# Attention and a two-layer GELU network on one core: second layers ordered behind the next first layer, and zero products in two waits of TensorE

## The chip, the cores and the metric

The kernel runs on one core of a Trainium2 chip. Five engines work side by side: TensorE (PE: products, and PEld: its weight loads), VectorE (DVE), ScalarE (ACT), GpSimd (POOL) and SyncE (SP, which starts most of the DMAs). The metric is the device time of one execution in microseconds (us); less is better.

## The reference, cut to what matters

```python
# attention: batch 4, 8 heads, 768 positions, head size 64; local window 96, 8 global columns
scores = scale * q @ k.T + bias            # masked to local or global positions
a = exp(scores - max) ; a = a / (sum(a) + 1e-9)
x = (a @ v)  -> [3072 tokens, 512]
# network
h = x @ w_in                               # [3072, 2048]
g = 0.5 * h * (1.0 + erf(h / sqrt(2)))
out = g @ w_out                            # [3072, 512]
```

## The kernel before, in words

The 3072 tokens are cut into 12 chunks of 256, three to a batch. The 2048 hidden columns are cut into 8 slices of 256. A step is one pair (chunk, slice); `STEPS` lists 99 entries: first the two first chunks in turn slice by slice, with three empty entries for a delay, then (2, 0) to (2, 7), (3, 0) and so on to (11, 7). The weights come in as 64-bit words and are taken apart on ScalarE and VectorE during the first two chunks, so that stage is crowded; later chunks find the weights split in a high and a low part in SBUF.

One step has a first layer (`m1`, lines 489, 493, 495: sixteen products in two halves f = 0, 1, of 128x512 and 128x256), a reduction of its bank on VectorE (line 497), two GELU passes on ScalarE for a high part `gh` and an exact value `gr` (lines 516, 517), the low part `gl` on VectorE (line 177), and a second layer (`m2`, line 536: twelve products of 512 columns, six for each half k of the tokens, adding to `acc` in PSUM). After slice 7 ScalarE copies `acc` out (line 549) and starts the DMA to HBM.

The attention of a later chunk runs between these steps: `scores_pair` (line 347), `exps`, `flip` (transposes, line 398, then ScalarE copies them to `pt`, line 402) and `av_pair` (line 430), whose result goes through ScalarE and VectorE into `x`, as a high and a low part; the low part is the last one written.

The loop in `run` emits for each T, in this order: the flag (at T = 91 alone), loads, `m1` of step T + 1 with its GELU, the transposes, the values, the scores, `m2` of step T, and the exponentials. This order is a priority and not the final order. A planner simulates the engines and puts each engine's instructions in a queue: at each moment the first ready one in the order of the code. Each engine then runs its queue in that order on the chip. `after(ins, prev, why)` adds an edge for the planner alone: `ins` comes behind `prev`. `behind` does so for VectorE, behind the last reduction or `gl` so far. Banks of PSUM for scores, transposes, values, first layers and the flag come from one pool of six (`bank`), and each is taken when the planner places the first instruction that writes it.

The flag (lines 622 to 645) is a small check of the inputs' range. Its last steps are three comparisons on VectorE, placed by `behind` after the `gl` of step 91, that is (11, 0); a reduction (line 639); and a transpose on TensorE into a bank (line 641). `warm` (line 366) puts products with zeros (`wz`) on TensorE at the start and between the scores of the first chunks; their results are read by nobody.

Of the kernel before, what the change touches and what calls it, by code (L numbers as in the profile page):

```python
# [17 lines left out]
P = 128  # L18
# [3 lines left out]
NP = H // 2  # L22
# [9 lines left out]
NST = 8  # L32
# [18 lines left out]
DECODE.update({(1, i): i - 1 for i in range(4)})  # L51
DECODE.update({(s, i): 2 * s - 2 + i // 2 for s in range(2, NST) for i in range(4)})
FILL = {(0, 0, 0): 8, (0, 0, 1): 5, (0, 1, 1): 9, (0, 2, 1): 4, (0, 3, 1): 4, (1, 0, 1): 4}
LATE = 6
CAT = 2
NEGMASK = -1000000000.0
# [30 lines left out]
class Fast:  # L87
# [107 lines left out]
    def split_weights(self, s, i):  # L195
        nc = self.nc
        if i == 0:
            if s == LATE:
                self.early.close()
# [120 lines left out]
    def scores_pair(self, c, p):  # L320
# [9 lines left out]
        for j in range(2):  # L330
            for a in range(1 if c == 0 and j == 0 else 2):
                for hh in range(2):
# [17 lines left out]
                    prev = ins  # L350
            if (c, p, j) in FILL:
                prev = self.warm(FILL[c, p, j], prev)
        for hh in range(2):
# [7 lines left out]
                self.last_dve = ins.ins  # L361
            self.pt_n[c, 2 * p + hh] = nn

    def warm(self, n, prev=None):
        for i in range(n):
            ins = self.nc.tensor.matmul(self.warm_ps, lhsT=self.wz[:, 0:P], rhs=self.wz, start=True, stop=True).ins  # L366
            if prev is not None:
                self.after(ins, prev, "between the products of the first attention")
            prev = ins
        return prev  # L370
# [22 lines left out]
    def flip(self, c, h):  # L393
        nc = self.nc
        nn = self.pt_n.pop((c, h))
        tp = self.bank([P, 3, P], f"t{c}_{h}")
        for i, o in enumerate((0, 2 * P, NK if c % CPB == 0 else P)):
            nc.tensor.transpose(tp[:, i, :], nn[:, o:o + P], self.ident)  # L398
        if h % 2 == 0:
            self.ptp2 = self.ptp.tile([P, 2, 3, P], F32, name=f"pt{c}_{h}", tag="pt")  # L400
        pt = self.ptp2[:, h % 2]
        nc.scalar.copy(pt, tp)  # L402
        self.pt_t[c, h] = pt

    def av_pair(self, c, p):

        nc = self.nc
        first = c % CPB == 0
        if p == 0:
            self.x[c] = self.xp.tile([P, NP, 2, CT], F32R, name=f"x{c}", tag="x")  # L410
        if c:
            if p % 2 == 0:
                return
            ps = range(p - 1, p + 1)
        else:
            ps = range(p, p + 1)
        n = len(ps)
        quarters = c > CAT
        if quarters:
            rows = [self.bank([P, 2, n, P], f"av{c}_{p}_{r}") for r in range(2)]  # L420
        elif first:
            avb = self.bank([P, 2, n, P], f"av{c}_{p}")
            av = [avb[:, j] for j in range(2)]
        else:
            av = [self.bank([P, n, P], f"av{c}_{p}_{j}") for j in range(2)]
        heads = {(i, hh): (self.pt_t.pop((c, 2 * q + hh)), self.vr[c][:, :, (2 * q + hh) * D:(2 * q + hh + 1) * D])
                 for i, q in enumerate(ps) for hh in range(2)}

        def add(out, lhs, rhs, start, stop):
            ins = nc.tensor.matmul(out, lhsT=lhs, rhs=rhs, start=start, stop=stop, skip_group_check=True).ins  # L430
            if self.last_av is not None:
                self.after(ins, self.last_av, "heads and halves in turn")
            self.last_av = ins

        for i in range(n if quarters else 0):
            for j in range(2):
                for r in range(2):
                    ks = slice(r * HQ, (r + 1) * HQ)
                    for hh in range(2):
                        pt, vt = heads[i, hh]  # L440
                        add(rows[r][hh * D:(hh + 1) * D, j, i, :], vt[ks, j, :], pt[ks, j, :],
                            i == 0 and j == 0, r == 1 and (first or j == 0) or r == 0 and j == 1 and not first)
        for i in range(0 if quarters else n):
            for j in range(2):
                for hh in range(2):
                    pt, vt = heads[i, hh]
                    add(av[j][hh * D:(hh + 1) * D, i, :], vt[:, j, :], pt[:, j, :],
                        i == 0 and (j == 0 or not first), first and j == 0)
        for i in range(n):
            for a in range(2):  # L450
                for j in range(2):
                    if first and j == 0:
                        continue
                    ks = slice(0, HQ) if first else slice(j * HQ, (j + 1) * HQ)
                    for hh in range(2):
                        pt, vt = heads[i, hh]
                        qs = slice(a * HQ, (a + 1) * HQ)
                        o = rows[0 if first else j][:, j] if quarters else av[j]
                        add(o[hh * D:(hh + 1) * D, i, qs], vt[ks, 2 + a, :], pt[ks, 2, qs], False, True)
        if quarters:  # L460
            xs = self.sm.tile([P, 2, n, P], F32, name=f"xs{c}_{p}", tag="o", bufs=3)
            nc.scalar.copy(xs, rows[1])  # L462
            nc.vector.tensor_tensor(out=xs, in0=rows[0], in1=xs, op=ALU.add)
            xh, xl = (self.x[c][:, ps.start:ps.stop, e].rearrange("d p (j q) -> d j p q", j=2) for e in range(2))
            nc.scalar.copy(xh, xs)
            self.lo_dve(xl, xs, xh)
            return
        if first:
            xh, xl = (self.x[c][:, ps.start:ps.stop, e].rearrange("d p (j q) -> d j p q", j=2) for e in range(2))
            nc.scalar.copy(xh, avb)  # L470
            self.lo_dve(xl, avb, xh)
            return
        for j in range(2):
            xh, xl = (self.x[c][:, ps.start:ps.stop, e, j * P:(j + 1) * P] for e in range(2))
            nc.scalar.copy(xh, av[j])
            self.lo_dve(xl, av[j], xh)

    def m1(self, t, f):
        nc = self.nc
        c, s = STEPS[t]  # L480
        x = self.x[c]
        wh, wl = self.win[s]
        fs = slice(f * P, (f + 1) * P)
        if c >= CAT:
            if f == 0:
                self.h[t] = self.hs.tile([P, 2, CT], F32, name=f"hs{t}", tag="hs")
            hp = self.bank([P, 2, CT], f"h{t}_{f}")
            for d in range(NP):
                nc.tensor.matmul(hp.rearrange("p e t -> p (e t)"), lhsT=wh[:, d, fs],  # L489
                                 rhs=x[:, d].rearrange("p e t -> p (e t)"),  # L490
                                 start=d == 0, stop=d == NP - 1, skip_group_check=True)
                if d:
                    nc.tensor.matmul(hp[:, 0, :], lhsT=wl[:, d - 1, fs], rhs=x[:, d - 1, 0, :],  # L493
                                     start=False, stop=False, skip_group_check=True)
            nc.tensor.matmul(hp[:, 0, :], lhsT=wl[:, NP - 1, fs], rhs=x[:, NP - 1, 0, :],  # L495
                             start=False, stop=True, skip_group_check=True)
            self.last_dve = nc.vector.tensor_reduce(out=self.h[t][:, f, :], in_=hp.rearrange("p e t -> p t e"),  # L497
                                                    axis=mybir.AxisListType.X, op=ALU.add).ins
            return
        if f == 0:  # L500
            self.h[t] = self.bank([P, 2, CT], f"h{t}")
        hp = self.h[t]
        n = 0
        for d in range(NP):
            for w, e in ((wh, 0), (wh, 1), (wl, 0)):
                nc.tensor.matmul(hp[:, f, :], lhsT=w[:, d, fs], rhs=x[:, d, e, :],  # L506
                                 start=n == 0, stop=n == 3 * NP - 1)
                n += 1
# [12 lines left out]
    def m2(self, t, k):  # L521
        nc = self.nc
        c, s = STEPS[t]
        gh, gl = self.g[t]
        wh, wl = self.wout[s]
# [5 lines left out]
        acc = self.acc[c, k]  # L531
        ks = slice(k * P, (k + 1) * P)
        n = 0
        for f in range(2):
            for g, w in ((gh, wh), (gh, wl), (gl, wh)):
                nc.tensor.matmul(acc, lhsT=g[:, f, ks], rhs=w[:, f, :],  # L536
                                 start=s == 0 and n == 0, stop=s == NST - 1 and n == 5)
                n += 1
        if s == NST - 1:
            o = self.sm.tile([P, DM], F32, name=f"o{c}_{k}", tag="o", bufs=3)  # L540
# [281 lines left out]
```

## Time and profile before

| | |
|---|---|
| Time, median of 3 runs | 683.29 us (682.39 to 683.58) |
| The profiled execution | 682.04 us |
| its span, from the first to the last instruction | 680.2 us |
| TensorE busy, weight loads | 665.6 us (98%), 561.5 us (83%) |
| VectorE, ScalarE, GpSimd busy | 390.3, 364.6, 102.4 us (57%, 54%, 15%) |
| Chain that ended last | PE 94%, DVE 3%, ACT 2% |
| Mean granted clock of TensorE | 0.997 of full speed |

Times within the trace are counted from the first instruction. Products overlap in the pipeline of TensorE: what one costs in a stream is the distance from its start to the next start, which is less than its listed duration. In a row of instructions in order of time the first number is the start, the second the duration of the row (of all its instructions together), and a bracket at the end gives the idle time ahead of it and what ended that.

### The profile page before, as it was taken

The numbers are of one execution on the slowest core, as the hardware profiler recorded it, in microseconds if no ns is written. First come the engines' busy times: TensorE is split into PE (matmuls) and PEld (weight loads), VectorE is DVE, ScalarE is ACT, GpSimd is POOL, SyncE is SP. The second block draws the span as 40 slices with busy tenths as digits, with TensorE's granted clock in tenths as the row PEclk, the third lists the DMA queues.
The fourth block names the chain that finished last, engine by engine and source line by source line (L and its number), as shares of the span: only waits on it lengthen the run. The fifth ranks groups of instructions, "written<-read, shape, count | busy, mean of one in ns | idle before, by whom it ended". The sixth has DMA issues, their size and how long they took to land.

```text
span 680.2 us, 13571 instructions
## 1 busy us (share of the span) xinstructions
PE 665.6 (98%) x5215; PEld 561.5 (83%) x5215; DVE 390.3 (57%) x1136; ACT 364.6 (54%) x852; POOL 102.4 (15%) x232
## 2 busy tenths in 40 slices
PE   8989999999999999999999999999999999999996
PEld 6658898988888888888888888888888888888784
DVE  5989989334555654655555555555546555453432
ACT  3796687554654645536636537446456356363211
POOL 3100330310301301301201121031031031010000
PEclk9999999999999999999999999999999999999998
DMA  8945944241531613403514324224154052000001
GB/s 267 276 147 186 290 152 125 79 125 47 164 94 62 164 35 122 140 29 113 126 41 153 97 67 156 69 72 140 32 132 135 24 161 64 32 1 16 16 1 36
DMA packets 66183, 71.21 MB, mean 105 GB/s; under 512 B 32704, under 2 KB 49344, under 8 KB 66112
## 3 DMA queue, kind: packets, MB, share of 16 engines
q1 hardware_dynamic: 61664, 62.93, 30.6%
q10 hardware_dynamic: 4448, 7.34, 3.1%
q8 instruction: 43, 0.70, 0.4%
q14 instruction: 28, 0.23, 0.1%
HBM read 63.97 MB, written 6.29 MB: 103 GB/s over the span
## 4 chain that ended last, share of the span: by engine, by line
PE 94%; DVE 3%; ACT 2%; issue 0%; DVEq 0%
PE acc L536 40%; PE h L489 22%; PE h L493 8%; PE h L506 6%; PE av L430 5%; PE s L347 5%; PE t L398 4%; PE h L495 3%; PE warm_ps L366 1%; DVE n L358 1%; DVE n L388 1%; ACT w L209 0%; ACT n L379 0%; DVE wb L217 0%; ACT L516 0%
## 5 line engine op out<-in xcount | busy, mean ns | idle before, releaser
L489 PE MATMUL h<-x,winh 128*128 128x512 f32 x640 | 216.3, 400 | 0.0
L497 DVE TENSOR_REDUCE hs<-h 128x256 f32<-128x512 f32 x160 | 107.7, 685 | 99.5 <-PE h L495 98.9
L536 PE MATMUL acc<-wouth,gh 128*128 128x512 f32 x384 | 156.8, 408 | 2.2 <-ACT gh L516 2.2
L536 PE MATMUL acc<-woutl,gh 128*128 128x512 f32 x384 | 150.3, 392 | 0.0
L536 PE MATMUL acc<-wouth,gl 128*128 128x512 f32 x384 | 148.5, 393 | 0.1
L388 POOL TENSOR_SCALAR n<-n,su 128x192 f32<-128x192 f32 (+1 forms) x160 | 71.3, 464 | 438.3 <-ACT n L379 217.9
L177 DVE TENSOR_TENSOR gl<-gr,gh 128x512 fp32r<-128x512 f32 x96 | 67.5, 703 | 117.6 <-ACT gr L517 117.6
L493 PE MATMUL h<-x,winl 128*128 128x256 f32 x480 | 134.7, 281 | 0.0
L489 PEld LDWEIGHTS h<-x,winh 128*128 128x128 f32 x640 | 114.2, 188 | 20.4 <-issue 0.3
L516 ACT ACTIVATE gh<-hs 128x512 fp32r<-128x512 f32 x80 | 50.7, 633 | 125.6 <-DVE hs L497 122.1
L402 ACT COPY pt<-t 128x384 f32<-128x384 f32 x96 | 45.4, 479 | 112.8 <-PE t L398 109.5
L493 PEld LDWEIGHTS h<-x,winl 128*128 128x128 f32 x480 | 90.4, 188 | 7.2
L536 PEld LDWEIGHTS acc<-wouth,gh 128*128 128x128 f32 x384 | 72.2, 188 | 21.0 <-ACT xs L462 3.9
L536 PEld LDWEIGHTS acc<-wouth,gl 128*128 128x128 f32 x384 | 72.1, 188 | 17.0 <-issue 0.6
L536 PEld LDWEIGHTS acc<-woutl,gh 128*128 128x128 f32 x384 | 72.3, 188 | 12.3
L379 ACT ACTIVATE n<-n,mn 128x192 f32<-128x192 f32 (+1 forms) x144 | 62.3, 434 | 1.4 <-DVE mn L358 1.2
L358 DVE CUSTOM_DVE_ANT_0 n<-s,pen 128x192 f32<-128x192 f32 (+1 forms) x192 | 54.6, 340 | 2.2 <-PE s L347 2.2
L517 ACT ACTIVATE gr<-hs 128x512 f32<-128x512 f32 x80 | 49.3, 616 | 0.0
L506 PE MATMUL h<-x,winh 128*128 128x256 f32 x256 | 48.9, 286 | 0.4 <-ACT x L470 0.2
L398 PE MATMUL t<-ident,n 128*128 128x128 f32 x288 | 47.2, 274 | 1.2 <-DVE n L388 1.2
L430 PE MATMUL av<-pt,vr 64*64 64x64 f32 (+2 forms) x1312 | 42.8, 249 | 2.7 <-ACT pt L402 2.6
L495 PE MATMUL h<-x,winl 128*128 128x256 f32 x160 | 45.2, 282 | 0.0
(87 smaller groups left out, 738.2 us busy)
## 6 DMA issues: line engine op xcount, KB each, us to landing
w<-w SPq DMA_DIRECT2D x32, 512.0 KB, 5.0
c<-w SPq DMA_DIRECT2D x32, 512.0 KB, 5.3
out<-o ACTq DMA_DIRECT2D x23, 256.0 KB, 2.0
qr<-qT SPq DMA_DIRECT2D x11, 512.0 KB, 3.9
vr<-v SPq DMA_DIRECT2D x22, 256.0 KB, 4.2
kr<-kT SPq DMA_DIRECT2D x16, 320.0 KB, 5.0
vr<-v SPq DMA_DIRECT2D x19, 192.0 KB, 2.8
kr<-kT SPq DMA_DIRECT2D x36, 64.0 KB, 4.1
```

The lines of the kernel that those rows point to most:

```text
L177: return self.nc.vector.tensor_tensor(out=out, in0=in_, in1=hi.bitcast(F32), op=ALU.subtract)
L358: ins = nc.vector.tensor_tensor_reduce(out=nn[:, j * NK:j * NK + n], in0=sp[hh][:, j, 0:n], in1=pen, scale=-slope(2 * p + hh), scalar=3e38 ...
L379: self.table(nc.scalar.activation(out=nn, in_=nn, func=AF.Exp, bias=mn[:, i:i + 1], scale=-1.0, accum_out=su[:, i:i + 1]))
L388: ins = eng.tensor_scalar(out=nn, in0=nn, scalar1=su[:, i:i + 1], scalar2=0.0, op0=ALU.mult, op1=ALU.add)
L398: nc.tensor.transpose(tp[:, i, :], nn[:, o:o + P], self.ident)
L430: ins = nc.tensor.matmul(out, lhsT=lhs, rhs=rhs, start=start, stop=stop, skip_group_check=True).ins
L489: nc.tensor.matmul(hp.rearrange("p e t -> p (e t)"), lhsT=wh[:, d, fs], rhs=x[:, d].rearrange("p e t -> p (e t)"), start=d == 0, stop=d == ...
L493: nc.tensor.matmul(hp[:, 0, :], lhsT=wl[:, d - 1, fs], rhs=x[:, d - 1, 0, :], start=False, stop=False, skip_group_check=True)
L495: nc.tensor.matmul(hp[:, 0, :], lhsT=wl[:, NP - 1, fs], rhs=x[:, NP - 1, 0, :], start=False, stop=True, skip_group_check=True)
L497: self.last_dve = nc.vector.tensor_reduce(out=self.h[t][:, f, :], in_=hp.rearrange("p e t -> p t e"), axis=mybir.AxisListType.X, op=ALU.ad ...
L506: nc.tensor.matmul(hp[:, f, :], lhsT=w[:, d, fs], rhs=x[:, d, e, :], start=n == 0, stop=n == 3 * NP - 1)
L536: nc.tensor.matmul(acc, lhsT=g[:, f, ks], rhs=w[:, f, :], start=s == 0 and n == 0, stop=s == NST - 1 and n == 5)
```

## The change

Three edits. (1) For second layers of chunks from 3 on, the first product of each half k is ordered behind the last first-layer product of the following step. (2) In the values of pair 3 of chunk 0, three products of zeros are put into the bank, behind the transposes before. (3) In the transposes of head 6 of chunk 1, two products of zeros are put into the bank, behind the transposes of head 5. The zeros are overwritten by the products that follow in the same bank.

```diff
+FILL_T = {(1, 6): 2}
+FILL_AV = {(0, 3): 3}
...
+    def zeros(self, n, out):
+        prev = self.last_t
+        for i in range(n):
+            ins = self.nc.tensor.matmul(out, lhsT=self.wz[:, 0:P], rhs=self.wz[:, 0:out.shape[1]],
+                                        start=True, stop=True, skip_group_check=True).ins
+            self.after(ins, prev, "behind the transposes of the head before")
+            prev = ins
...
         tp = self.bank([P, 3, P], f"t{c}_{h}")
+        if (c, h) in FILL_T:
+            self.zeros(FILL_T[c, h], tp.rearrange("k i q -> k (i q)"))
         for i, o in enumerate((0, 2 * P, NK if c % CPB == 0 else P)):
-            nc.tensor.transpose(tp[:, i, :], nn[:, o:o + P], self.ident)
+            self.last_t = nc.tensor.transpose(tp[:, i, :], nn[:, o:o + P], self.ident).ins
...
             avb = self.bank([P, 2, n, P], f"av{c}_{p}")
             av = [avb[:, j] for j in range(2)]
+            if (c, p) in FILL_AV:
+                self.zeros(FILL_AV[c, p], avb.rearrange("d j n q -> d (j n q)"))
...
-            nc.tensor.matmul(hp[:, 0, :], lhsT=wl[:, NP - 1, fs], rhs=x[:, NP - 1, 0, :],
-                             start=False, stop=True, skip_group_check=True)
+            self.last_m1 = t, nc.tensor.matmul(hp[:, 0, :], lhsT=wl[:, NP - 1, fs], rhs=x[:, NP - 1, 0, :],
+                                               start=False, stop=True, skip_group_check=True).ins
...
             for g, w in ((gh, wh), (gh, wl), (gl, wh)):
-                nc.tensor.matmul(acc, lhsT=g[:, f, ks], rhs=w[:, f, :],
-                                 start=s == 0 and n == 0, stop=s == NST - 1 and n == 5)
+                ins = nc.tensor.matmul(acc, lhsT=g[:, f, ks], rhs=w[:, f, :],
+                                       start=s == 0 and n == 0, stop=s == NST - 1 and n == 5).ins
+                if n == 0 and c > CAT and self.last_m1[0] == t + 1:
+                    self.after(ins, self.last_m1[1], "behind the first layer of the next step")
                 n += 1
```

## Rows read from the trace of the kernel before

**Rows 1.** The page: busy us, share of the span and count, TensorE alone.

```profile
...
PE 665.6 (98%) x5215; PEld 561.5 (83%) x5215; DVE 390.3 (57%) x1136; ACT 364.6 (54%) x852; POOL 102.4 (15%) x232
...
```

**Rows 2.** Waits of TensorE, whole span: who for whom, us, times, longest.

```profile
...
PE av L430 <- ACT pt L402: 2.6, 3, 1.3
PE acc L536 <- ACT gh L516: 2.2, 2, 1.4
...
```

**Rows 3.** Waits of TensorE from 0 to 62 us.

```profile
...
PE acc L536 <- ACT gh L516: 0.8, 1, 0.8
...
```

**Rows 4.** TensorE in order of time around the last wait.

```profile
...
624.22 0.63 PE L489 MATMUL h<-x,winh 128*128 128x512 f32 x2
...
625.38 0.40 PE L536 MATMUL acc<-wouth,gh 128*128 128x512 f32 x1
...
629.68 0.27 PE L495 MATMUL h<-x,winl 128*128 128x256 f32 x1
...
631.40 0.50 PE L536 MATMUL acc<-wouth,gh 128*128 128x512 f32 x1 [1.45 <-ACT gh L516]
...
634.60 0.27 PE L641 MATMUL flag_ps<-ident,bad 128*1 128x128 f32 x1
634.63 0.71 PE L489 MATMUL h<-x,winh 128*128 128x512 f32 x2
...
```

**Rows 5.** VectorE and ScalarE in order of time, the same stretch.

```profile
...
623.81 0.69 DVE L177 TENSOR_TENSOR x<-xs,x 128x512 fp32r<-128x512 f32 x1 [0.69 <-ACT x L465]
...
628.36 0.59 ACT L549 COPY o<-acc 128x512 f32<-128x512 f32 x1 [0.79 <-PE acc L536]
...
630.71 0.63 ACT L516 ACTIVATE gh<-hs 128x512 fp32r<-128x512 f32 x1 [1.77 <-DVE hs L497]
...
631.90 0.69 DVE L177 TENSOR_TENSOR gl<-gr,gh 128x512 fp32r<-128x512 f32 x1 [1.22 <-ACT gr L517]
...
632.81 0.16 DVE L639 TENSOR_REDUCE bad<-ok 128x1 f32<-128x5 f32 x1
...
```

**Rows 6.** TensorE and VectorE in order of time, an undisturbed step.

```profile
...
659.73 0.63 PE L489 MATMUL h<-x,winh 128*128 128x512 f32 x2
...
662.41 0.28 PE L495 MATMUL h<-x,winl 128*128 128x256 f32 x1
662.53 0.40 PE L536 MATMUL acc<-wouth,gh 128*128 128x512 f32 x1
...
664.64 0.69 DVE L177 TENSOR_TENSOR gl<-gr,gh 128x512 fp32r<-128x512 f32 x1 [1.22 <-ACT gr L517]
...
665.27 0.61 PE L489 MATMUL h<-x,winh 128*128 128x512 f32 x2
...
```

**Rows 7.** In order of time, chunk boundary 3 to 4, the first of five.

```profile
...
252.65 0.69 DVE L177 TENSOR_TENSOR x<-xs,x 128x512 fp32r<-128x512 f32 x1
...
255.30 0.40 PE L536 MATMUL acc<-wouth,gh 128*128 128x512 f32 x1
...
```

**Rows 8.** TensorE in order of time, the first chunks.

```profile
...
1.46 5.49 PE L366 MATMUL warm_ps<-wz 128*128 128x512 f32 x12 [1.46 <-DVE wz L572]
...
12.25 2.35 PE L366 MATMUL warm_ps<-wz 128*128 128x512 f32 x9
...
30.00 0.43 PE L430 MATMUL av<-pt,vr 128*64 128x128 f32 x2 [1.33 <-ACT pt L402]
30.36 0.88 PE L347 MATMUL s<-kr,qr 64*64 64x192 f32 x16
...
47.59 0.76 PE L398 MATMUL t<-ident,n 128*128 128x128 f32 x4 [1.19 <-DVE n L388]
...
```

**Rows 9.** Three stretches: length, busy us of each engine, granted clock (PEclk), DMA.

```profile
core 0: us, PE busy (x) PEld busy (x) DVE busy (x) ACT busy (x) POOL busy (x), PEclk, DMA share, GB/s
28.00:30.00 2.00, 0.67 (x5) 0.35 (x5) 2.00 (x6) 2.00 (x8) 0.00 (x0) 1.00 0.96 291
46.00:48.00 2.00, 0.81 (x6) 0.51 (x5) 1.97 (x8) 2.00 (x8) 0.00 (x0) 1.00 0.00 0
30.00:40.00 10.00, 9.52 (x95) 7.08 (x96) 9.99 (x39) 8.48 (x19) 0.00 (x0) 1.00 0.80 305
```

## The prediction, made before the changed kernel was run

> **What bounds the kernel now.** I read the page's busy table first, then the waits of TensorE, then its instructions in order of time around each wait, then the other engines beside those. The reader is to see in the busy table that TensorE is occupied for 665.6 us, 98% of the span [rows 1]. So time can leave only in three ways: TensorE gets less to do, its instructions follow each other more tightly, or one of its waits goes. The change takes no product away, so it comes down to the waits and to the places beside them. The waits are few: three for copied probabilities (2.6 us together), two of a second layer for its GELU (2.2 us together) [rows 2], one of 1.19 us before a head's transposes [rows 8], and the start. In the first 62 us a GELU is waited for once, for 0.8 us [rows 3]; the list of waits from 60 to 620 us is empty. So one wait is left behind the first stage, the 1.45 us before 631.40 in the last chunk [rows 4].
>
> The profiled execution took 682.04 us, of which 680.2 are the span; the median of the three timed runs is 683.29, so 1.25 above it. I make the sum against 682.04 and carry that offset along.
>
> **The tie, where the order changes.** With step numbers t over all (chunk, slice) pairs, the tie asks that the second layer of t starts behind the last product of the first layer of t + 1. From the fourth chunk on the stream of TensorE already has that order nearly everywhere. I find it broken at six chunk boundaries: at five, two or three of the twelve second-layer products stand in the middle of the next chunk's first layer; at the sixth (chunk 10 to chunk 11), all twelve.
>
> The first of the five is at 255.30. There TensorE has no gap, so moving two products behind ten costs and brings nothing, provided that the first layer's inputs are there when it is no longer interrupted. The low half of x is written by 253.34 (252.65 + 0.69) and needed at 255.30 [rows 7], so 1.96 us to spare: cost 0. What fails if that cover goes is a wait of the same size as the delay, five times.
>
> **The sixth boundary, where time is to be had.** In the kernel before, the first layer of (11, 0) stops after six products at 625.38, twelve second-layer products of (10, 7) run, then the other ten; the last is issued at 629.68 [rows 4]. Now TensorE has nothing left that the order allows: the next second layer is that of (11, 0) itself, whose GELU can only start now (630.71 [rows 5]). It starts at 631.40, runs in two halves, and the next thing (the transpose of the flag) is issued at 634.60 [rows 4]. Without trouble the first product would have followed 0.12 us after 629.68 (662.41 to 662.53) and the twelve would take 2.74 us (662.53 to 665.27) [rows 6]. So this place costs 634.60 - 629.80 - 2.74 = 2.06 us, of which 1.45 is the wait that the list names and the rest is the slow start and a second stop for gl.
>
> With the tie the first layer of (11, 0) runs in one piece: 2.80 us (659.73 to 662.53 [rows 6]) from 624.22, so to 627.02. The low half of x is there at 624.50 [rows 5] and wanted at 625.38: 0.88 us to spare. Then the twelve products of (10, 7), to 629.76, and beside them the reduction and the GELU of (11, 0). In an undisturbed step gl is complete 2.92 us after the last first-layer product (662.41 to 665.33 [rows 6]); here that is 626.90 + 2.92 = 629.82.
>
> What is late next is the flag. The code asks for the flag's bank before the banks of the first layer of (11, 1), and the stream shows that banks are given out in the order of the code: the flag's transpose at 634.60, then that first layer at 634.63 [rows 4]. The transpose is queued on TensorE ahead of the first layer of (11, 1), and by the tie ahead of the second layer of (11, 0) as well; both wait for it. It needs the flag's last reduction on VectorE, which is ordered behind gl and ended 0.38 us after it (632.59 to 632.97 [rows 5]). So it is ready at about 630.20, and TensorE is free at 629.76: a wait of 0.44 us, with 0.16 for the signal and the slow start after a stop (an estimate: a quarter of the 0.61 by which this place now costs more than its wait) 0.6 us in all. From there on first and second layers alternate without a wait, as in the step of [rows 6]. **Gain of the tie: 2.06 - 0.6 = 1.46 us.** Its bounds: 2.06 if the flag is in time, and a loss if the GELU is not in time (rivals). The output copies of chunk 10 move some 1.6 us later with their second layer; they and their DMA on ScalarE's queue are waited for by nobody near. No load moves, and nothing is passed on the queues of SP or POOL.
>
> **The products with zeros.** Three of 256 columns go into the bank of the fourth pair's values in chunk 0, behind the last transposes; the wait there is 28.67 to 30.00. Two of 384 columns go into the bank for head 6 of chunk 1; the wait there is 46.40 to 47.59 [rows 8]. A zero product of 512 columns takes 2.35 / 9 = 0.26 us [rows 8]; by that the three cost at most 0.78 and the two at most 0.52, and both fit into their waits. If either bank is not free by then, the products go onto the path: +1.3 us is the upper end. At both moments the scores of the pair before have been read out and at most four of the six banks are held (the two transposes' and values not yet copied), so I take 0.
>
> Below nothing: taking the bank early also lets the tiles behind it take theirs. After the wait the two value products come first and the sixteen scores of the next pair right behind (30.00, 30.36 [rows 8]); with the bank taken at 28.7 the scores may run inside the wait, which would give back at most their 0.88 us. But in the stretch after it VectorE is busy 9.99 of 10 us [rows 9], so an earlier score mostly makes a longer later wait. Between 0 and 0.88 I take the end near VectorE's full row: **-0.2 us**.
>
> As for the clock: the granted clock is 1.00 in both waits [rows 9], the upper of its two levels (2.4 GHz), so in this execution the zeros keep up nothing that had fallen. The Trainium skill ("TensorE: Matmul & The Clock Gate", Part 1, on what is actually happening) says that the throttled state is the default and activity releases it, and that one kernel shows different counts of slow first products from run to run. By that the timed runs may hold a fall which this profile does not show; no row here has one. It is a rival below.
>
> **Sum.** 682.04 - 1.46 - 0.2 = 680.4 for a profiled execution; with the offset of 1.25, a median of 681.6 us.
>
> **The rivals.**
> *The wait changes its name.* ScalarE takes the first output copy of chunk 10 ahead of the GELU of (11, 0). That copy can start 0.24 us after its six products (628.36 against 625.38 + 2.74 for the later one [rows 4, 5]), so at 627.02 + 1.37 + 0.24 = 628.63, ending 629.22; from GELU start to complete gl is 1.88 us (630.71 to 632.59), then 0.38 for the flag: 631.48. The wait is 1.72 + 0.16, the gain 0.2: 683.1. For it: before, both copies stood ahead of that GELU. Against: there it became ready long after them; now its input is there first and it stands first in the code.
> *Slower.* Both copies ahead of it: the second ends at 629.76 + 0.24 + 0.59 = 630.59, gl at 632.47, flag 632.85; TensorE waits 3.09 + 0.16 = 3.25 us where it lost 2.06, with the second layer that used to fill the time now tied behind. The kernel gets 1.2 us slower: 684.5. It decides from the point where the flag is ready later than 631.66.
> *The timed runs lose clock in the first waits, and the zeros stop that.* At the lower level twelve products take 5.49 us, 0.46 each, against 0.26 [rows 8]; 2.8 us of products issued at that level would be the whole offset of 1.25. Then the median comes down by it too: 681.6 - 1.2 = 680.4. For it: two of the three runs stand 1.2 and 1.5 us above the profiled one. Against: every row of the granted clock there.
> *The zeros don't get into their waits*, or shift the order of the crowded first 60 us: +1.3 on the sum, 682.9.
>
> **How the numbers follow.** Forecast 0.52 (681.6, its own range 680.8 to 682.4), first rival 0.15, slower 0.09, clock 0.12, zeros outside 0.12. A measurement of this kernel tells a change from none at about 0.2%, here 1.4 us: faster means below 681.9, slower above 684.7. Of the forecast about 0.37 lies below 681.9, with the clock rival all but 0.01: faster 0.48. Slower by 0.2% takes the slow rival with something of the zeros or a bad median: 0.06. The rest, 0.46, is within. The range 680.1 to 683.5 leaves out most of the slow rival and the ends of the others.
>
> **What would show it.** Right: the second layers of the last chunk no longer list the 1.45 us wait for gh; the first layer of (11, 0) is in one piece from 624; TensorE's wait there is about half a microsecond and names the flag's transpose. Wrong: that transpose waits over 1.5 us; a first layer waits for x at a boundary; the two waits at 28.7 and 46.4 have grown, or a zero product stands behind their end; TensorE's count of waits between 60 and 620 us is no longer none.

## The result, and the profile after

The changed kernel took 685.73 us in the median of eight runs (685.07 to 689.07), the kernel before 683.02 (eight runs, 682.39 to 683.88): ratio 1.0053, 95% interval 1.004 to 1.0066, so by the ratio 3.6 us slower (the medians alone are 2.7 us apart, since three of the eight runs lie some 3 us above the other five). The forecast was 681.6, range 680.1 to 683.5: wrong in sign and outside its range. The eight runs form two groups, five from 685.07 to 686.00 and three from 688.08 to 689.07. The profiled execution, 688.08 with a span of 686.2, is of the upper group and shows both losses.

TensorE's row of the page hardly changed from [rows 1]: the change added no work worth speaking of.

```profile
...
PE 667.2 (97%) x5220; PEld 564.0 (82%) x5220; DVE 389.3 (57%) x1136; ACT 365.2 (53%) x852; POOL 113.8 (17%) x232
...
```

TensorE's waits in the whole span (who for whom, us in total, times, longest) did change.

```profile
...
PE s L349 <- POOL qr L173: 3.2, 1, 3.2
PE t L410 <- DVE n L398: 2.2, 3, 1.4
PE h L520 <- ACT x L489: 1.8, 1, 1.8
PE h L520 <- DVE x L179: 1.5, 2, 1.2
...
PE acc L550 <- ACT gh L530: 1.2, 2, 0.7
PE flag_ps L657 <- DVE bad L655: 1.1, 1, 1.1
PE av L444 <- ACT pt L414: 0.7, 1, 0.7
```

The two targets shrank against [rows 2]: `pt` from 2.6 to 0.7, `gh` from 2.2 to 1.2. The third, for `n`, grew from 1.2 to 2.2 in three pieces. New are the flag's and, 6.5 us together, those for `x` and `qr`: tiles that the diff doesn't touch.

Where the time goes is read from the starts of first layers, counted in both traces in order of time (us):

| | before | after | difference |
|---|---|---|---|
| first of the 24-product groups of chunks 0 and 1 | 31.17 | 29.50 | -1.67 |
| third | 55.07 | 52.26 | -2.81 |
| fourth | 60.47 | 63.58 | +3.11 |
| seventh | 79.18 | 82.27 | +3.09 |
| eighth | 85.85 | 93.88 | +8.03 |
| step (2, 0) | 148.60 | 156.18 | +7.57 |
| step (11, 0) | 624.22 | 631.74 | +7.52 |
| step (11, 5) | 654.17 | 660.80 | +6.62 |

The kernel is ahead until 55 us, loses around 58 and again around 88, carries 7.5 us unchanged through nine chunks, and gets 0.90 back in the last chunk. The -2.81 overstates the lead, because six products of the third group now stand ahead of value products that came before it: chunk 1's last value products end at 54.90 and not at 55.14, with those six products (0.8 us) already done, so the lead is about 1.0 us. From there to +3.11 the first place costs about 4.1 us; the second costs 8.03 - 3.09 = 4.94. So there are three places to read.

**First place.** TensorE in order of time from 27.5 us: the zeros lie inside the old wait, and the rest closed up behind them. The sixteen scores and the next first layer now run before the values, which no longer wait (in [rows 8] the order was 1.33 us of wait, values, scores).

```profile
...
28.16 0.60 PE L369 MATMUL av<-wz 128*128 128x256 f32 x3
28.69 0.88 PE L349 MATMUL s<-kr,qr 64*64 64x192 f32 x16
29.50 0.50 PE L520 MATMUL h<-x,winh 128*128 128x256 f32 x2
...
30.76 0.92 PE L444 MATMUL av<-pt,vr 128*64 128x128 f32 x12
```

Some 25 us later ScalarE's order differs. Before (lines L475 and L229 there), then after (L489, L231, L211):

```profile
...
55.17 0.65 ACT L475 CAST x<-av 128x256 fp32r<-128x256 f32 x2 [1.71 <-PE av L430]
55.70 0.64 ACT L229 CAST winh<-wb 128x512 fp32r<-128x512 f32 x1
...
```

```profile
...
54.93 0.37 ACT L489 CAST x<-av 128x256 fp32r<-128x256 f32 x1 [1.91 <-PE av L444]
55.20 0.62 ACT L231 CAST winh<-wb 128x512 fp32r<-128x512 f32 x1
55.72 0.68 ACT L211 ACTIVATE w<-w 128x512 int32<-128x512 uint32 x1
56.28 0.37 ACT L489 CAST x<-av 128x256 fp32r<-128x256 f32 x1
...
```

Two instructions on weights now stand between the two copies of chunk 1's last values, and on VectorE four others stand before the second low part (55.68 to 57.81). TensorE's queue waits for both:

```profile
...
56.71 0.39 PE L520 MATMUL h<-x,winh 128*128 128x256 f32 x1 [1.81 <-ACT x L489]
58.28 0.58 PE L520 MATMUL h<-x,winh 128*128 128x256 f32 x1 [1.19 <-DVE x L179]
...
62.55 0.50 PE L550 MATMUL acc<-wouth,gh 128*128 128x512 f32 x1 [0.69 <-ACT gh L530]
...
```

The granted clock falls in the same stretch. Windows of after (length, busy us of PE, PEld, DVE, ACT, POOL, granted clock, DMA), then of before:

```profile
...
55.00:60.00 5.00, 2.10 (x9) 1.90 (x10) 4.77 (x11) 3.02 (x7) 0.00 (x0) 0.78 0.47 188
60.00:65.00 5.00, 4.31 (x27) 3.93 (x27) 3.55 (x7) 4.22 (x7) 0.00 (x0) 0.88 0.90 312
85.00:90.00 5.00, 1.75 (x19) 1.25 (x17) 3.14 (x6) 3.40 (x6) 4.85 (x4) 0.85 1.01 373
90.00:95.00 5.00, 5.00 (x26) 4.08 (x23) 4.68 (x15) 0.00 (x0) 0.00 (x0) 0.81 0.32 130
...
```

```profile
...
55.00:60.00 5.00, 4.11 (x37) 3.53 (x27) 4.98 (x12) 4.80 (x9) 0.00 (x0) 1.00 0.57 231
60.00:65.00 5.00, 5.00 (x35) 4.65 (x34) 5.00 (x11) 3.51 (x7) 0.00 (x0) 1.00 0.88 280
85.00:90.00 5.00, 5.00 (x47) 4.35 (x46) 5.00 (x15) 2.00 (x4) 0.00 (x0) 1.00 1.04 333
...
```

Before, all of these are at 1.00, the upper of the two levels (2.4 GHz). What the fall costs is read from the products: the fourteen from 58.28 take 2.94 us to the next start, the fourteen from 71.03, at 1.00 again, 1.67. So the first place is made of waits of 1.81 and 1.19 us and some 1.3 us of slower products, which is about what it costs.

**Second place.** GpSimd scales chunk 2's queries, before and then after:

```profile
...
72.24 5.40 POOL L171 TENSOR_SCALAR qr<-qr,qsc 128x256 f32<-128x256 f32 x4 [52.11 <-DMA qr<-qT]
```

```profile
...
71.92 17.93 POOL L173 TENSOR_SCALAR qr<-qr,qsc 128x256 f32<-128x256 f32 x4 [52.12 <-DMA qr<-qT]
```

The same four instructions take 17.93 us instead of 5.40, 16.57 of them for the first, and TensorE's scores wait 3.25 us for them. TensorE in after, then the same products in before:

```profile
...
88.54 1.77 PE L349 MATMUL s<-kr,qr 64*64 64x192 f32 x16 [3.25 <-POOL qr L173]
...
92.04 0.39 PE L550 MATMUL acc<-woutl,gh 128*128 128x512 f32 x1
...
```

```profile
...
82.14 0.88 PE L347 MATMUL s<-kr,qr 64*64 64x192 f32 x16
...
84.00 0.40 PE L536 MATMUL acc<-woutl,gh 128*128 128x512 f32 x1
...
```

From the scores to that product of the second layer it is 3.50 us instead of 1.86, while the granted clock is low: 3.25 + 1.64 = 4.89, nearly all of the second place's 4.94. VectorE runs without a gap from 63.02 to 88.14 in after; in before it pauses for 0.80 us just ahead of 72.12. The Trainium skill ("SBUF — State Buffer", SBUF: two separate sides) has VectorE and GpSimd share one pair of ports as an exclusive lock: of a VectorE instruction in a two-port mode, or with two inputs in SBUF, and a GpSimd instruction, the one that starts first holds the pair for the whole instruction, and the other blocks. The direction agrees with 17.93 against 5.40; which of VectorE's instructions hold it no run here separates.

**Third place.** TensorE in the last chunk, which answers to [rows 4]:

```profile
...
631.74 0.63 PE L503 MATMUL h<-x,winh 128*128 128x512 f32 x2
...
634.44 0.28 PE L509 MATMUL h<-x,winl 128*128 128x256 f32 x1
...
637.07 0.39 PE L550 MATMUL acc<-wouth,gl 128*128 128x512 f32 x1
638.53 0.27 PE L657 MATMUL flag_ps<-ident,bad 128*1 128x128 f32 x1 [1.08 <-DVE bad L655]
...
```

The first layer is in one piece, twelve second-layer products follow, and the only wait is the flag's. VectorE, answering to [rows 5]:

```profile
...
636.67 0.69 DVE L179 TENSOR_TENSOR gl<-gr,gh 128x512 fp32r<-128x512 f32 x1 [1.22 <-ACT gr L531]
637.28 0.27 DVE L644 TENSOR_SCALAR ok<-nn 128x1 f32<-128x1 f32 x3
637.47 0.21 DVE L651 CAST wmin<-wand 128x128 f32<-128x128 int32 x1
637.72 0.29 DVE L652 TENSOR_REDUCE mx<-wmin 128x1 f32<-128x128 f32 x1
638.04 0.15 DVE L653 TENSOR_SCALAR ok<-mx 128x1 f32<-128x1 f32 x1
638.23 0.16 DVE L655 TENSOR_REDUCE bad<-ok 128x1 f32<-128x5 f32 x1
...
```

`gl` is complete at 637.36 and the flag's reduction at 638.39: 1.03 us apart, where it was 0.38 before. Three more small instructions of the flag (L651 to L653) now stand behind `gl` too. Before, they ran 7 us ahead of it, from here on:

```profile
...
624.53 0.23 DVE L635 CAST wmin<-wand 128x128 f32<-128x128 int32 x1
...
```

### The profile page after: what moved, and what is told of

Its sections match the earlier page's. It is cut to its first block, busy times and chain, and to the rows that moved or that the text cites. A ratio compares the mean times of both kernels' runs of the same rounds, so it can differ in the third digit from the quotient of the medians.

```text
span 686.2 us, 13575 instructions
## 1 busy us (share of the span) xinstructions
PE 667.2 (97%) x5220; PEld 564.0 (82%) x5220; DVE 389.3 (57%) x1136; ACT 365.2 (53%) x852; POOL 113.8 (17%) x232
## 4 chain that ended last, share of the span: by engine, by line
PE 91%; DVE 2%; POOL 2%; ACT 2%; issue 1%; DMA 1%; SPq 0%; POOLq 0%
PE acc L550 37%; PE h L503 22%; PE h L507 8%; PE av L444 5%; PE h L520 5%; PE s L349 5%; PE t L410 4%; PE h L509 3%; POOL qr L173 2%; PE warm_ps L376 2%; ACT n L389 1%; DMA qr<-qT 1%; DVE n L398 0%; DVE n L360 0%; DVE wb L221 0%
## 5 line engine op out<-in xcount | busy, mean ns | idle before, releaser
L507 PE MATMUL h<-x,winl 128*128 128x256 f32 x480 | 134.7, 281 | 0.0
L503 PEld LDWEIGHTS h<-x,winh 128*128 128x128 f32 x640 | 114.0, 188 | 20.2 <-issue 0.3
L173 POOL TENSOR_SCALAR qr<-qr,qsc 128x256 f32<-128x256 f32 x48 | 38.6, 820 | 61.7 <-DMA qr<-qT 61.7
L520 PEld LDWEIGHTS h<-x,winh 128*128 128x128 f32 x256 | 41.7, 195 | 6.1 <-DVE x L179 2.4
```

What stands on the lines that cost most here:

```text
L173: self.nc.gpsimd.tensor_scalar(out=out, in0=in_, scalar1=scale, scalar2=0.0, op0=ALU.mult, op1=ALU.add)
```

## The experiments

The theory after the result: the tie gains about 0.9 us, and the three zeros in the values cause the whole loss, by changing the order that the planner writes in the first stage. Rivals: the tie harms something; the zeros harm as work on TensorE; what counts is that the bank is taken early.

**The tie alone.**
```diff
-FILL_T = {(1, 6): 2}
-FILL_AV = {(0, 3): 3}
+FILL_T = {}
+FILL_AV = {}
```


> The tie alone, no zero products. Theory (the tie gains what the tail of the changed trace shows, and all of the loss lies in the first 100 us): 0.9 us faster than before, about 682.1; no fall of the granted clock before 100 us; first step of chunk 2 at the same instant as before (148.6 us) within 0.5. Rival (tie and zeros only cost together, or the tie disturbs the first chunks too): 683 to 686.

682.34 us (680.03 to 682.92, 12 runs), ratio 0.9984 [0.9971, 0.9996]: 1.1 us faster (0.3 to 2.0). The early order is that of before; the flag's wait of 1.1 us is there. The tie isn't what costs. In this trace and in six others that have the tie and the flag where it was, 0.85 to 0.88 us come back between step (11, 0) and step (11, 5). Two parts of the theory missed: the profiled execution has falls of the clock before 100 us, and its first step of chunk 2 starts 1.6 us later than before. Its runs fall in two groups by mean granted clock: five at 0.996 to 0.999 took 680.03 to 681.46, seven at 0.992 or 0.993 took 682.28 to 682.92. The profiled one is of the second group; its windows show where:

```profile
...
30.00:35.00 5.00, 5.00 (x49) 3.77 (x50) 4.86 (x20) 3.78 (x12) 0.00 (x0) 0.75 0.98 382
...
50.00:55.00 5.00, 5.00 (x32) 4.36 (x28) 5.00 (x9) 2.07 (x5) 0.00 (x0) 0.70 0.33 97
...
```

TensorE ran busy at 0.75 and 0.70, behind the very two waits into which the change puts zeros. Of the 24 runs of the kernel before beside these (median 682.60), sixteen were at 0.995 or more (681.42 to 683.17) and eight below (683.21 to 684.23).

**The zeros alone.**
```diff
-                if n == 0 and c > CAT and self.last_m1[0] == t + 1:
+                if False:
```


> Both sets of zero products, no tie. Theory: the whole loss and none of the gain: 2.7 + 0.9 = 3.6 us slower than before, about 686.6, with two falls of the clock before 100 us. Rival (the zeros cost only together with the tie): as before, 683.

689.96 us (685.99 to 690.51, 6 runs), ratio 1.008 [1.0055, 1.0106]: the loss comes with the zeros, with the same waits for `qr` (3.2) and `x` (1.8 and 1.5). By the ratio it is 5.5 us and not 3.6: two runs, 685.99 and 686.38, are near the theory's 686.6, the other four at 689.68 or above. Without the tie nothing comes back in the last chunk: 8.64 us behind the kernel before at step (11, 0), 8.69 at (11, 5).

**Tie, and zeros in the values only.**
```diff
-FILL_T = {(1, 6): 2}
+FILL_T = {}
```


> The tie and the three zero products in the values of chunk 0 alone. Theory (taking that bank early lets the sixteen scores go ahead and re-orders what VectorE and ScalarE do next): as the changed kernel, 685 to 688. Rival (the two in the transposes of chunk 1 do it): as the tie alone, 682.1.

686.63 us (685.04 to 691.82, 7 runs), ratio 1.0078 [1.0045, 1.011]: the theory holds. The profiled execution (685.27) has the waits for `x` and a clock of 0.50 from 60 to 65 us, but no wait for `qr`, although VectorE's queue around it is in the order of the changed kernel:

```profile
...
72.14 9.04 POOL L173 TENSOR_SCALAR qr<-qr,qsc 128x256 f32<-128x256 f32 x4 [52.55 <-DMA qr<-qT]
...
```

So the second place is not lost in every execution.

**Tie, and zeros in the transposes only.**
```diff
-FILL_AV = {(0, 3): 3}
+FILL_AV = {}
```


> The tie and the two zero products in the transposes of chunk 1 alone. Theory: they lie wholly inside the 1.2 us wait and re-order nothing, so as the tie alone, 682.1. Rival (they do the harm): 685 to 688.

681.93 us (680.73 to 683.19, 12 runs), ratio 0.9989 [0.9978, 0.9999]. The order is that of before but for the two products, and they lie in their wait (1.19 us in [rows 8]):

```profile
...
45.30 0.59 PE L369 MATMUL t<-wz 128*128 128x384 f32 x2
...
46.66 0.85 PE L410 MATMUL t<-ident,n 128*128 128x128 f32 x4 [0.77 <-DVE n L398]
...
```

So these two cost nothing, and the whole loss hangs on the three in the values.

**The three zeros at the same place, but into the bank of `warm`,** so that the bank of the values isn't taken early (no zeros in the transposes).
```diff
-                self.zeros(FILL_AV[c, p], avb.rearrange("d j n q -> d (j n q)"))
+                self.zeros(FILL_AV[c, p], self.warm_ps[:, 0:2 * P])
```


> The tie, and the three zero products at the same place of TensorE's queue but into the bank of the warm-up, so that the values' bank is not taken early and the sixteen scores stay behind the first value products. Theory 1 (the early bank and the scores that go ahead do the harm): as the tie alone, 682.3. Rival (any few tenths of a microsecond put into TensorE's queue there make the planner interleave ScalarE's and VectorE's work otherwise, above all a weight copy between the two copies of chunk 1's last values): 685 to 689, with the wait of a first layer for x at 55 to 58 us.

687.98 us (685.77 to 689.09, 6 runs), ratio 1.0075 [1.0056, 1.0094]. Values and scores keep the order of before, and the values still wait; the loss is there all the same. TensorE, then ScalarE:

```profile
...
28.48 0.60 PE L369 MATMUL warm_ps<-wz 128*128 128x256 f32 x3
30.04 0.43 PE L444 MATMUL av<-pt,vr 128*64 128x128 f32 x2 [0.96 <-ACT pt L414]
...
```

```profile
...
56.57 0.37 ACT L489 CAST x<-av 128x256 fp32r<-128x256 f32 x1 [2.27 <-PE av L444]
56.84 0.62 ACT L231 CAST winh<-wb 128x512 fp32r<-128x512 f32 x1
57.36 0.68 ACT L211 ACTIVATE w<-w 128x512 int32<-128x512 uint32 x1
57.93 0.37 ACT L489 CAST x<-av 128x256 fp32r<-128x256 f32 x1
...
```

My theory that the early bank does it fell. Three products, 0.60 us together, in TensorE's queue are enough for the planner to write another order 25 us later. In this profiled execution (687.72) nothing waits for `qr`: the 7.0 us by which it is behind at 79 us are lost around 58, with the clock at 0.50 from 60 to 65.

**The changed kernel with chunk 1's last copies pinned ahead of the weight slices.** `x_copied` is None until the last copy is emitted.
```diff
         ins = nc.scalar.copy(hi, af).ins
+        if self.x_copied is not None:
+            self.after(ins, self.x_copied, "behind the last copies of chunk 1's values")
...
-            nc.scalar.copy(xh, av[j])
-            self.lo_dve(xl, av[j], xh)
+            xi = nc.scalar.copy(xh, av[j]).ins
+            xj = self.lo_dve(xl, av[j], xh).ins
+            if (c, p, j) == (1, 3, 1):
+                self.x_copied, self.last_dve = xi, xj
```


> The changed kernel, with two edges more for the planner: the copies of chunk 1's last values on ScalarE and VectorE come ahead of the weight slices after them, as they stood in the kernel before. Theory (the wait of 1.8 + 1.2 us for x at 55 to 58 us, and the fall of the clock behind it, are the larger part of the loss): the wait is gone or under 0.5 us, 3 us or more come back, 682 to 683, below the kernel before by what the tie gains if no other wait appears. Rival (the loss lies elsewhere, in the queries of chunk 2): 685 or more, with the wait for x gone.

684.77 us (683.60 to 685.95, 12 runs), ratio 1.0029 [1.0019, 1.0039]. TensorE's waits from 50 to 100 us:

```profile
...
PE s L352 <- POOL qr L174: 3.6, 1, 3.6
PE acc L555 <- ACT gh L535: 1.8, 1, 1.8
...
```

The wait for `x` there shrinks to 0.7 (the theory had under 0.5), and the first place is repaired: at the seventh group the kernel stands at -0.10 against before, where the changed kernel stood at +3.09. The GELU starts at 58.70 as before (58.79); TensorE, which is earlier, waits 1.8 us for it. `qr` stays, and 5.40 us are lost there. By the ratios, repairing one place gives back 1.6 of 3.6 us; the theory's 682 to 683 was missed because the other place remains.

**The changed kernel with chunk 2's queries scaled on VectorE.**
```diff
+        if c == 2:
+            self.nc.vector.tensor_scalar(out=qr[:, p], in0=qr[:, p], scalar1=self.qsc[:, p:p + 1], scalar2=0.0,
+                                         op0=ALU.mult, op1=ALU.add)
+        else:
+            self.hi_pool(qr[:, p], qr[:, p], self.qsc[:, p:p + 1])
```


> The changed kernel, with the scaling of chunk 2's queries on VectorE and not on GpSimd. Theory (GpSimd's 16.6 us instruction, held up while VectorE never pauses, makes TensorE wait 3.2 us in the slower group of runs): the slower group is gone, all runs at 684.5 to 686, the wait for qr is gone, the wait for x at 55 to 58 us stays. Rival (the two groups come from the clock alone): two groups as before, 685 and 688.5.

685.36 us (683.63 to 686.05, 8 runs), ratio 1.0033 [1.0019, 1.0048]. No wait for `qr`, and no run above 686.05; nothing is lost at the second place (+5.35 against before at the seventh group and at the eighth). With the wait in the profile of the upper group, this says that the upper group of the changed kernel was this wait; that only three of its eight runs were in that group leaves some room for chance. Two runs, at 683.63 and a mean clock of 0.996, are below the theory's range. The waits for `x` stay at 1.8 and 1.5.

**Both repairs,** the two edits above together, on the changed kernel.
```diff
+        if self.x_copied is not None:
+            self.after(ins, self.x_copied, "behind the last copies of chunk 1's values")
...
+        if c == 2:
+            self.nc.vector.tensor_scalar(out=qr[:, p], in0=qr[:, p], scalar1=self.qsc[:, p:p + 1], scalar2=0.0,
+                                         op0=ALU.mult, op1=ALU.add)
...
```


> The changed kernel with both repairs at once: the weight slices behind the last copies of chunk 1's values, and chunk 2's queries scaled on VectorE. Theory (the loss is these two waits and the clock that falls in them, and nothing else): what is left is the tie's gain of 0.9 us, so 682.1 where the kernel before has 683.0, ratio 0.9987; TensorE's waits for x under 0.8 us each, none for qr. Rival (with three zeros in the queue the order of the whole first stage is another, and the repairs only move the lost time to the next late result): TensorE waits for gh in chunk 1 for 2 us or more, as with the copies alone, and the time stays at 684 or above, ratio 1.0015 to 1.003.

683.03 us (681.50 to 683.74, 11 runs) beside 682.48, ratio 1.0005 [0.9995, 1.0015]. Neither theory's number: the repairs give back 3.3 of the 3.6 us, but not the tie's gain. At the seventh and the eighth group the kernel is 2.33 us behind the kernel before. The longest wait left from 50 to 100 us is one for `gh`, and the clock is low behind it (the wait, then the window):

```profile
...
PE acc L559 <- ACT gh L539: 1.8, 1, 1.8
...
```

```profile
...
60.00:65.00 5.00, 4.71 (x23) 4.53 (x24) 5.00 (x10) 4.01 (x8) 0.00 (x0) 0.66 0.47 143
...
```

**The tie with the flag's transpose two steps later** (no zeros).
```diff
-        bp = self.bank([P, 512], "flag_ps")
+        self.bad = bad
+
+    def flag_end(self, flag_i):
+        nc, sm, bad = self.nc, self.const, self.bad
+        bp = self.bank([P, 512], "flag_ps")
...
                 self.flag(flag_i)
+            if T == last - 6:
+                self.flag_end(flag_i)
```


> The tie alone, and the flag's transpose put two steps after the flag's work on VectorE. Theory (what is left of the tie's gain is lost in the 1.1 us wait of the flag's transpose): that wait is gone, 1.1 us less than the tie alone (682.3), about 681.2, 2 us less than before. Rival (a first layer or second layer then waits for the same GELU): as the tie alone.

680.86 us (678.18 to 681.89, 12 runs) beside 683.03, ratio 0.9968 [0.9956, 0.998]: faster than both kernels. From step (10, 7), 618.69 against 616.91, to (11, 5), 653.87 against 654.17, its starts move from +1.77 to -0.30 against before: 2.07 us, the upper bound of the prediction for this place (2.06). The list of TensorE's waits has no flag any more.

**The same, with the two zeros in the transposes.**
```diff
 FILL_T = {(1, 6): 2}
-FILL_AV = {(0, 3): 3}
+FILL_AV = {}
...
+            if T == last - 6:
+                self.flag_end(flag_i)
```


> The tie with the flag's transpose two steps later, plus the two zeros in the transposes of head 6 of chunk 1; no zeros in the values. Theory (these two zeros lie inside their wait and cost nothing, and bring nothing): as without them, 680.9 where the kernel before has 683.0, ratio 0.9969. Rival (the zeros keep TensorE at the higher level of its clock in more of the runs): the share of runs with a mean granted clock of 0.995 or more goes up, and the time is 679.5, ratio 0.995. Second rival (the first stage's order shifts as with the zeros in the values): 684 or more.

680.74 us (679.94 to 681.46, 8 runs) beside 682.48, ratio 0.9973 [0.9962, 0.9983]. No difference from the kernel without them that can be told, and again 2.07 us in the last chunk. Five of the eight runs have a mean clock of 0.995 or more, seven of twelve without the zeros: the rival that they hold up the clock finds no support in these runs.

## Why the prediction was wrong, point by point

**The step that failed: the zeros, "I take 0", then -0.2.** That they fit into their waits was right: three at 28.16, two at 45.30 in the kernel that has these alone. Wrong was to price them as work at their place, with +1.3 as the upper end. In this kernel an edit also goes into the planner, and the order of everything behind it comes out anew. By their ratios the tie alone brings 1.1 us and the zeros alone cost 5.5 (3.8 to 7.2): the second is outside my bounds by some 4 us. The runs showed in its place a new order on ScalarE and VectorE, with waits of 1.81 and 1.19 us for `x`, in some executions one of 3.25 for `qr`, and a lower clock behind them; repairing the two places gives back 3.3 us. The rival "shift the order of the crowded first 60 us" had the mechanism with chance 0.12 and the wrong size, and it ended at 60 us: the second loss, 4.94 us in the profiled execution, stands at 88. The text's own row said that VectorE is busy 9.99 of 10 us from 30 to 40 [rows 9]. In this stage a changed order moved TensorE by whatever came late.

**The guess on the early bank** went half right: the scores did run inside the wait, and at the next first layer the kernel was ahead by 1.67 us, or 1.3 without the two value products that now come later. That is more than the 0.88 of the text. Most of it was gone 8 us later, in waits of 0.34, 0.52 and 0.51 us, as the text had said ("an earlier score mostly makes a longer later wait"). What it didn't have is that the copies of `x`, 25 us later, come later than before.

**The tie's term, 1.46, measured 0.90.** Its parts up to the flag hit: the first layer took 634.44 + 0.12 - 631.74 = 2.82 us (forecast 2.80), `gl` came 2.92 us after the last first-layer product (forecast 2.92). The mis-sized part is the wait for the flag: forecast 0.44 and 0.16, measured 1.08 and about 0.15. I counted the comparisons and the last reduction behind `gl`, as in [rows 5], and not the three steps (0.65 us) that before had finished earlier. With the flag moved out of the way the place gave the whole 2.07, so the rest of this mechanism is shown.

**The five other boundaries:** cost 0, right; no wait of TensorE between 92 and 620 us. Of the text's signs of being wrong, two came: TensorE waits between 60 and 620 us again (0.69 at 62.55, 3.25 at 88.54), and the second of the two targeted waits grew, from 1.19 to 1.44.

**The rivals on the output copies** ("changes its name", "slower") didn't occur: the GELU of (11, 0) came ahead of both copies.

**The rival on the clock** was right about the timed runs of before; for the zeros no run shows the gain. Runs of before at a mean clock below 0.995 take about 1.7 us more than the others (medians 684.0 and 682.3 of the 24 runs), which would account for the offset of 1.25 between the profiled execution and the median that I only carried along; the clock of those three timed runs is not on record. But the two zeros that change no order change nothing measurable; for the three others a gain by the clock can't be told from the loss. The profiles leave room for it: from 30 to 35 us the clock is 1.00 in all seven with the three zeros, in two of the five without. The price of the lower level was read from the first 7 us, where the windows show a clock of 1.00; where the changed kernel has a recorded fall, products of 512 columns start 0.42 us apart (91.27 to 91.69) and not 0.46, against 0.23 behind it. In the changed kernel the falls stand right behind its new waits and cost some 1.3 and 1.6 us; that the waits cause them is likely but not shown, since the run with the copies pinned has a wait of 1.8 us there and no fall.

**Still open:** which comparison of the planner tips when the three zeros are added was not followed. That the order differs and that the two repairs give back 3.3 of 3.6 us is shown, the tipping step isn't; each repair is an edit that goes into the planner as well. Nor was followed why the tie puts the flag's three small steps behind `gl`.

## What to carry to other kernels

Where a planner writes the order, price an edit twice: at its place, and as a new draw of the order in every crowded stage behind it; make the range as wide as that draw, and pin the few orders that matter before adding filler. When a wait is removed, walk back through everything queued ahead of the next late instruction, also what was early before. A gain found in one part of a bundle (here 2.07 us in the tie, with the flag moved) is worth isolating, since the other part may hide it.

## What was not expected of the hardware

Four GpSimd instructions of 128x256 took 5.26 to 5.45 us in the five profiles in which VectorE had paused for 0.80 to 0.83 us shortly before them, 9.04 and 9.76 in two others, and 16.48 to 17.93 in the three in which VectorE did not pause until just before the first of the four ended. The order of VectorE's instructions alone doesn't decide it: 9.04 and 17.93 were measured beside the same order. Where the first of the four took long and a pause of VectorE is to be seen (four profiles), it ended 0.34 to 0.35 us after VectorE's last instruction ahead of the pause, and one such pause was of 0.06 us only.

And a wait of 1 to 4 us of TensorE in the first 100 us can cost more than itself: in ten of the twelve profiles the granted clock of a stretch of 5 us was found at its lowest between 0.50 and 0.78 behind one. The profiles of the kernel before and of the tie with the zeros in the transposes (flag where it was) show no fall in this stage, with waits of up to 1.33 us. The two groups of runs of the kernel before, 0.992 to 0.994 and 0.995 or more, say that the same kernel has falls in some executions and not in others, or more of them.
